# One decode step of an adaLN attention block: keys and values as one stream of 53 transfers, sums by transposes, the last wo row like the others

## The chip, the core and the metric

The kernel runs on one core of a Trainium2 chip. A core has a matrix engine (TensorE, "PE", with weight loads shown as "PEld"), a vector engine (VectorE, "DVE"), a scalar engine (ScalarE, "ACT"), a general engine (GpSimd, "POOL"), and a queue engine (SyncE, "SP") that here issues all transfers; 16 DMA engines move the data. The on-chip memory (SBUF) has 128 partitions; matmul results go to PSUM. The metric is the device time of one execution in microseconds, as the median of several. The profile shows one execution, from its first to its last instruction (its span).

## What is computed

One token (D = 640) goes through an adaptive-layernorm block: attention over a cache of 8192 positions with 32 heads of 192, then a squared-ReLU MLP with 1536 hidden units. All is fp32.

```python
mod = (silu(c) @ w_mod).reshape(6, 640)
sa, ca, ga, sb, cb, gb = mod
h = layernorm(x) * (1 + ca) + sa
q = (h @ wq).reshape(32, 192)
scores = einsum("hd,hkd->hk", q, k_cache) * 192 ** -0.5
o = einsum("hk,hkd->hd", softmax(scores), v_cache)
x = x + ga * (o.reshape(32 * 192) @ wo)
h = layernorm(x) * (1 + cb) + sb
x = x + gb * (relu(h @ w1 + b1) ** 2 @ w2 + b2)
```

The two caches are 201 MB each and every byte is read once; all weights together are some 49 MB.

## The kernel before

**Streaming.** Everything comes through three SBUF slots (`slot`, L54) of 14,208 words per partition, used in turn. A transfer into a slot waits until what was in it is used up. The order on SP is: the first weights `wm0`, then for each head its keys (`load_k`) and its values (`load_v`), then the remaining weights `wm1`, `w1`, `gb`, `w2` (L312 to L319). The keys of a head are 64 positions per partition, each of 192 words. Behind the keys of most heads lies a piece of weights in the same transfer: `wq` for the next pair of heads behind the even ones, `wo` of the pair before behind the odd ones. The last two heads' keys come in two and in four pieces (`CUTS`), the values of head 31 are behind the `wo` of the last pair.

**Keys** (`keys`, L192). For one half of a head's positions at a time, DVE multiplies the keys by the query that every partition holds (L201, in place); POOL folds the last 7/16 of the positions, adding the upper 96 words of each to the lower 96 (L203); DVE meanwhile sums the other 9/16 (L204), then the folded ones (L205). That gives one score per position.

**Softmax** (`softmax`, L216). DVE takes the maximum in each partition (L218), PE spreads it over all partitions by a matmul with the identity (L220), DVE takes the maximum of that (L222), and ACT computes the exponentials with their sum in each partition (L228). After an odd head PE adds the two heads' sums over the partitions with a matmul with ones (`total`, L97).

**Values** (`values`, L233). The positions go 8 at a time: 8 steps, each 3 matmuls of a 32-column group with 512 columns of values (L240). An fp32 matmul shows as two instructions in the profile, so a head is 48. The useful eighth of the result is picked by a mask in `project` (L254, L256), which one pair later also divides by the sum, and turns the row into columns by a matmul with `quad` (L258). `attend` (L260) multiplies it with the pair's piece of `wo`: 6 matmuls of 320 columns in two column groups, accumulated in `att_a` over the pairs; for the last pair 12 of 160 columns in four column groups, on top of `att_a` that `gather` (L275) had already brought into place while the keys of head 31 were still being worked on.

**The end.** The modulation rows 3 and 4 are computed by `mod` in steps, placed between the parts of the second layernorm (the `between` of `layernorm`, L107; `mod_b`, L326). Row 2 is done before the values of head 31 (L308). Then follow the first MLP matrix (L343), bias, ReLU and square (L346 to L348), the row 5 (`mod`, L351) and two rounds of matmuls whose result nobody reads (`WARM`, L353 to L355), the second MLP matrix (L363), and the result (L366 to L368).

All engines run their instructions in the order in which the program writes them.

Of the kernel before, what the change touches and what calls it, by code (L numbers as in the profile page):

```python
# [8 lines left out]
F32 = mybir.dt.float32  # L9
# [22 lines left out]
CUTS = {("k", H - 2): 2, ("k", H - 1): 4}  # L32
WO = 3 * D
WQ = KB * PW
HD = NPOS * DH
SLOT = HD + WO
WITHOUT_W = (1, H - 2)
WITH_W = tuple(h for h in range(H) if h not in WITHOUT_W)
W1_CUT = ((0, 3), (3, 2))
W2_CUT = ((0, 6), (6, 3), (9, 1), (10, 1), (11, 1))  # L40
WARM = 2
EPS = 1e-5


@with_exitstack
def block_kernel(ctx: ExitStack, tc: tile.TileContext, kw, ky, vc, wm0, wm1, w1, gb, w2, out):
# [18 lines left out]
    quad = const.tile([P, 32 * NV], F32, name="quad")  # L65
    nc.vector.memset(quad, 0.0)
    for g in range(NV):
        nc.vector.memset(quad[32 * g:32 * (g + 1), 32 * g:32 * (g + 1)], 1.0)
# [31 lines left out]
    def layernorm(x, copies, scale1, shift, name, between=lambda: None):  # L100
# [6 lines left out]
        between()  # L107
# [24 lines left out]
    def mod(first, n, w, steps=(KB,)):  # L132

        ps = psum.tile([P, 512], F32, tag="q", name=f"ps_mod{first}", bufs=2)
        b = 0
        for k in steps:
            for b in range(b, b + k):
                wb = w[:, b].rearrange("p (m n) -> p m n", m=n)
                for g in range(G):
                    nc.tensor.matmul(ps[32 * g:32 * (g + 1), :n * DG], e[:, b:b + 1].to_broadcast([P, 32]),  # L140
                                     wb[:, :, DG * g:DG * (g + 1)], start=(b == 0), stop=(b == KB - 1))
            b += 1
            if b < KB:
                yield
        nc.vector.tensor_copy(mods[:, first:first + n], ps[:, :n * DG].rearrange("p (m n) -> p m n", m=n))  # L145
        yield

    qb_t, k_t, v_t = {}, {}, {}

    def load(src, to, h, what):  # L150
        to[h] = slot(f"{what}{h}")
        n, w = CUTS.get((what, h), 1), src.shape[1]
        for c in range(n):
            a, b = c * HD // n, (c + 1) * HD // n if c + 1 < n else w
            nc.sync.dma_start(to[h][:, a:b], src[:, a:b])

    def load_k(h):

        load(kw[WITH_W.index(h)] if h in WITH_W else ky[WITHOUT_W.index(h)], k_t, h, "k")

    def load_v(h):
        load(vc[h], v_t, h, "v")

    load_k(0)
    next(mod(0, 2, wm0_t[:, :KB * 2 * D].rearrange("p (b n) -> p b n", b=KB)))
# [8 lines left out]
    hR = const.tile([P, KB, P], F32, name="hR")  # L174
    nc.vector.tensor_copy(hR, h1[:, :, None].to_broadcast([P, KB, P]))

    def query(i, w):
        w = w.rearrange("p (b n) -> p b n", b=KB)
        ps = psum.tile([P, 512], F32, tag="q", name=f"ps_q{i}", bufs=2)
        for b in range(KB):  # L180
            nc.tensor.matmul(ps[:, :PW], hR[:, b], w[:, b], start=(b == 0), stop=(b == KB - 1))  # L181
        qb_t[i] = work.tile([P, PW], F32, name=f"qb{i}", tag="qb")
        nc.scalar.activation(qb_t[i], ps[:, :PW], AF.Copy, scale=DH ** -0.5)  # L183
# [3 lines left out]
    att_s = const.tile([P, 2 * DG], F32, name="att_s")  # L187
    nc.vector.memset(att_s, 0.0)
    att_t = []
    query(0, wm0_t[:, KB * 2 * D:KB * 2 * D + WQ])  # L190

    def keys(h, between):  # L192

        q = qb_t[h // 2][:, DH * (h % 2):DH * (h % 2 + 1)]
        sc = work.tile([P, NPOS], F32, tag="sc", name=f"sc{h}")
        t = k_t[h][:, :HD].rearrange("p (i d) -> p i d", d=DH)
        n = NPOS // max(2, CUTS.get(("k", h), 1))
        m = n - POOL * n // 16
        for c in range(NPOS // n):
            pr, s = t[:, c * n:(c + 1) * n], sc[:, c * n:(c + 1) * n]  # L200
            nc.vector.tensor_mul(pr, pr, q[:, None, :].to_broadcast([P, n, DH]))  # L201
            half = pr[:, m:, :DH // 2]
            nc.gpsimd.tensor_add(half, half, pr[:, m:, DH // 2:])  # L203
            nc.vector.tensor_reduce(s[:, :m], pr[:, :m], axis=AX.X, op=ALU.add)  # L204
            nc.vector.tensor_reduce(s[:, m:], half, axis=AX.X, op=ALU.add)  # L205
            between(c)
        return sc
# [3 lines left out]
    def inverse(i):  # L211
        r = work.tile([P, 2], F32, tag="r", name=f"r{i}")
        nc.vector.reciprocal(r, sum_t.pop(i))
        ri_t[i] = r

    def softmax(h, sc):  # L216
        mp = work.tile([P, 1], F32, tag="mp", name=f"mp{h}")
        nc.vector.tensor_reduce(mp, sc, axis=AX.X, op=ALU.max)  # L218
        ps = psum.tile([P, 512], F32, tag="sm", name=f"ps_mx{h}", bufs=2)
        nc.tensor.matmul(ps[:, :P], mp.to_broadcast([P, P]), ident, start=True, stop=True)  # L220
# [3 lines left out]
        p = work.tile([P, NPOS, 32 // E], F32, tag="p", name=f"p{h}", bufs=1)  # L224
# [3 lines left out]
        nc.scalar.activation(p, sc[:, :, None].to_broadcast([P, NPOS, 32 // E]), AF.Exp, bias=nm, accum_out=sp[:, h % 2:h % 2 + 1])  # L228
        if h % 2:
            sum_t[h // 2] = total(sp, f"sum{h // 2}")  # L230
        return p

    def values(h, p):  # L233

        t = v_t.pop(h)[:, :HD].rearrange("p (j g n) -> p j g n", g=NV, n=E * ED)
        ps_t[h] = psum.tile([P, 512], F32, tag="o", name=f"ps_o{h}", bufs=3)
        n = NPOS // E
        for j in range(n):
            for g in range(NV):
                nc.tensor.matmul(ps_t[h][32 * g:32 * (g + 1)], p[:, E * j:E * (j + 1)].rearrange("p e r -> p (e r)"),  # L240
                                 t[:, j, g], start=(j == 0), stop=(j == n - 1))
# [3 lines left out]
    def project(i):  # L245
# [3 lines left out]
        inverse(i)  # L249
        r2 = ri_t.pop(i)  # L250
        for a in range(2):
            h = 2 * i + a
            om = work.tile([P, ED, E], F32, tag="om", name=f"om{h}", bufs=1)
            nc.vector.scalar_tensor_tensor(om[:n], ps_t.pop(h)[:n].rearrange("p (d e) -> p d e", e=E), r2[:n, a:a + 1],  # L254
                                           mask[:n, None, :].to_broadcast([n, ED, E]), op0=ALU.mult, op1=ALU.mult)
            nc.vector.tensor_reduce(os_[:n, a], om[:n], axis=AX.X, op=ALU.add)  # L256
        os_t[i] = psum.tile([P, 512], F32, tag="sm", name=f"ps_oT{i}", bufs=2)
        nc.tensor.matmul(os_t[i][:, :n], os_[:n].rearrange("p a d -> p (a d)"), quad[:n], start=True, stop=True)  # L258

    def attend(i, w):  # L260
        oT = work.tile([P, 96], F32, tag="oT", name=f"oT{i}")
        nc.vector.tensor_copy(oT, os_t.pop(i)[:, :96])  # L262
        w = w.rearrange("p (j n) -> p j n", j=3)
        if i + 1 < NPAIR:
            for j in range(3):
                for g in range(2):
                    nc.tensor.matmul(att_a[32 * g:32 * (g + 1), :2 * DG], oT[:, 32 * j:32 * (j + 1)],  # L267
                                     w[:, j, 2 * DG * g:2 * DG * (g + 1)], start=(i == 0 and j == 0), stop=(i == NPAIR - 2 and j == 2))
            return
# [141 lines left out]
```

## Time and profile before

| | |
|---|---|
| device time, median of 3 runs | 1057.9 us (1057.46 to 1057.91) |
| span of the profiled execution (its device time is not shown by itself) | 1055.5 us |
| DVE busy | 831.4 us (79%) |
| PE busy | 463.7 us (44%) |
| POOL busy | 194.8 us (18%) |
| bytes read from HBM | 451.82 MB |
| mean granted TensorE clock | 0.694 of full speed |

In the profile, a group of instructions is named by its line, its engine and what it writes and reads, with its count, busy time and the mean of one in ns. In the view of the stretches, the columns after the stretch are its length, the busy time (and number of instructions) of PE, PEld, DVE, ACT and POOL, the granted TensorE clock, the busy share of the DMA engines and the GB/s that they moved. In the timeline, a row is a start, the time until the last of its instructions ended, engine, line and operation, and in brackets the idle time before it and what ended that.

### The profile page before, as it was taken

The numbers are of one execution on the slowest core, as the hardware profiler recorded it, in microseconds if no ns is written. First come the engines' busy times: TensorE is split into PE (matmuls) and PEld (weight loads), VectorE is DVE, ScalarE is ACT, GpSimd is POOL, SyncE is SP. The second block draws the span as 40 slices with busy tenths as digits, with TensorE's granted clock in tenths as the row PEclk, the third lists the DMA queues.
The fourth block names the chain that finished last, engine by engine and source line by source line (L and its number), as shares of the span: only waits on it lengthen the run. The fifth ranks groups of instructions, "written<-read, shape, count | busy, mean of one in ns | idle before, by whom it ended". The sixth has DMA issues, their size and how long they took to land.

```text
span 1055.5 us, 5687 instructions
## 1 busy us (share of the span) xinstructions
PE 463.7 (44%) x2356; PEld 155.0 (15%) x2356; DVE 831.4 (79%) x409; ACT 33.4 (3%) x88; POOL 194.8 (18%) x72
## 2 busy tenths in 40 slices
PE   3234443355543345463334534335453335535446
PEld 1101111111111111120111111101111111111113
DVE  2886878978787987878888687997878798789963
ACT  1000000000000000000000000000000000000000
POOL 0211112211212221212221212221221221122110
PEclk9667666766666766666676666666666666767769
DMA  9999999999999999999999999999999999999997
GB/s 403 435 434 428 432 440 427 441 424 437 433 433 428 440 424 441 424 439 427 431 437 437 422 442 430 428 439 426 439 429 433 428 438 433 434 427 432 424 426 310
DMA packets 11410, 452.18 MB, mean 428 GB/s; under 512 B 1269, under 2 KB 1273, under 8 KB 1785
## 3 DMA queue, kind: packets, MB, share of 16 engines
q1 hardware_dynamic: 11384, 451.83, 99.3%
q8 instruction: 18, 0.29, 0.1%
q14 instruction: 8, 0.06, 0.0%
HBM read 451.82 MB, written 0.00 MB: 428 GB/s over the span
## 4 chain that ended last, share of the span: by engine, by line
DMA 42%; DVE 39%; PE 17%; ACT 1%; issue 1%; SPq 0%; DVEq 0%; ACTq 0%
DMA k<-in_kw 36%; DVE k L201 21%; PE ps_o L240 14%; DVE sc L204 12%; DVE sc L205 5%; DMA k<-in_ky 3%; DMA w_t<-in_w 2%; PE ps_mx L220 1%; DMA wm_t<-in_wm 1%; ACT p L228 1%; PE ps_sum L97 1%; PE ps_mod L140 1%; PE ps_q L181 1%; DVE nm L222 0%; DVE mp L218 0%
## 5 line engine op out<-in xcount | busy, mean ns | idle before, releaser
L201 DVE TENSOR_TENSOR k<-k,qb 128x6144 f32<-128x6144 f32 (+1 forms) x66 | 419.7, 6359 | 141.6 <-DMA k<-in_kw 134.4
L203 POOL TENSOR_TENSOR k<-k 128x1344 f32<-128x1344 f32 (+1 forms) x66 | 194.1, 2941 | 820.9 <-DVE k L201 476.1
L240 PE MATMUL ps_o<-v,p 128*32 128x512 f32 x1536 | 290.4, 731 | 17.2 <-ACT p L228 17.2
L204 DVE TENSOR_REDUCE sc<-k 128x18 f32<-128x3456 f32 (+1 forms) x66 | 240.5, 3644 | 4.3
L220 PE MATMUL ps_mx<-ident,mp 128*128 128x128 f32 x64 | 25.5, 501 | 416.2 <-DVE mp L218 416.2
L240 PEld LDWEIGHTS ps_o<-v,p 128*32 128x32 f32 x1536 | 68.4, 131 | 215.4 <-issue 193.1
L267 PE MATMUL att_a<-k,oT 128*32 128x320 f32 x180 | 49.6, 720 | 114.2 <-DVE oT L262 113.1
L205 DVE TENSOR_REDUCE sc<-k 128x14 f32<-128x1344 f32 (+1 forms) x66 | 99.0, 1500 | 0.0
L220 PEld LDWEIGHTS ps_mx<-ident,mp 128*128 128x128 f32 x64 | 16.1, 312 | 442.8 <-DVE mp L218 421.0
L181 PE MATMUL ps_q<-k,hR 128*128 128x384 f32 x150 | 52.3, 496 | 0.0
L228 ACT ACTIVATE p<-sc,nm 128x256 f32<-128x256 f32 x32 | 16.2, 508 | 760.6 <-DVE nm L222 496.9
L267 PEld LDWEIGHTS att_a<-k,oT 128*32 128x32 f32 x180 | 13.7, 161 | 136.7 <-DVE oT L262 116.7
L222 DVE TENSOR_REDUCE nm<-ps_mx 128x1 f32<-128x128 f32 x32 | 9.3, 291 | 28.5 <-PE ps_mx L220 28.5
L181 PEld LDWEIGHTS ps_q<-k,hR 128*128 128x128 f32 x150 | 27.3, 190 | 27.9 <-issue 11.7
L254 DVE SCALAR_TENSOR_TENSOR om<-ps_o,r,mask 96x512 f32<-96x512 f32 x32 | 23.9, 747 | 6.5 <-PE ps_o L240 5.4
L256 DVE TENSOR_REDUCE os<-om 96x64 f32<-96x512 f32 x32 | 21.8, 682 | 1.1
L140 PE MATMUL ps_mod<-wm_t,silu 128*32 128x320 f32 (+1 forms) x120 | 11.7, 550 | 14.6 <-DVE silu L128 14.6
L97 PE MATMUL ps_sum<-sp,ones 128*128 128x2 f32 x32 | 9.4, 364 | 17.2 <-ACT p L228 17.2
L183 ACT ACTIVATE qb<-ps_q 128x384 f32<-128x384 f32 x16 | 7.9, 491 | 195.2 <-PE ps_q L181 195.2
L97 PEld LDWEIGHTS ps_sum<-sp,ones 128*128 128x128 f32 x32 | 8.0, 312 | 21.9 <-ACT p L228 21.9
L145 DVE COPY mods<-ps_mod 128x320 f32<-128x320 f32 (+1 forms) x4 | 1.6, 398 | 10.2 <-PE ps_mod L140 10.2
L76 DVE COPY small<-wm_t 128x27 f32<-128x27 f32 x1 | 0.2, 179 | 11.2 <-DMA wm_t<-in_wm 11.2
(77 smaller groups left out, 90.9 us busy)
## 6 DMA issues: line engine op xcount, KB each, us to landing
k<-in_kw SPq DMA_DIRECT2D x29, 7104.0 KB, 27.4
v<-in_vc SPq DMA_DIRECT2D x32, 6144.0 KB, 22.1
k<-in_ky SPq DMA_DIRECT2D x1, 6144.0 KB, 28.3
k<-in_ky SPq DMA_DIRECT2D x2, 3072.0 KB, 21.5
k<-in_kw SPq DMA_DIRECT2D x3, 1536.0 KB, 15.5
wm_t<-in_wm SPq DMA_DIRECT2D x1, 4173.5 KB, 12.7
wm_t<-in_wm SPq DMA_DIRECT2D x1, 3200.0 KB, 29.3
wm_t<-in_wm SPq DMA_DIRECT2D x1, 2560.0 KB, 18.2
```

What stands on the lines that cost most here:

```text
L97: nc.tensor.matmul(ps[:, :n], ones, src, start=True, stop=True)
L140: nc.tensor.matmul(ps[32 * g:32 * (g + 1), :n * DG], e[:, b:b + 1].to_broadcast([P, 32]), wb[:, :, DG * g:DG * (g + 1)], start=(b == 0), s ...
L181: nc.tensor.matmul(ps[:, :PW], hR[:, b], w[:, b], start=(b == 0), stop=(b == KB - 1))
L201: nc.vector.tensor_mul(pr, pr, q[:, None, :].to_broadcast([P, n, DH]))
L203: nc.gpsimd.tensor_add(half, half, pr[:, m:, DH // 2:])
L204: nc.vector.tensor_reduce(s[:, :m], pr[:, :m], axis=AX.X, op=ALU.add)
L205: nc.vector.tensor_reduce(s[:, m:], half, axis=AX.X, op=ALU.add)
L220: nc.tensor.matmul(ps[:, :P], mp.to_broadcast([P, P]), ident, start=True, stop=True)
L228: nc.scalar.activation(p, sc[:, :, None].to_broadcast([P, NPOS, 32 // E]), AF.Exp, bias=nm, accum_out=sp[:, h % 2:h % 2 + 1])
L240: nc.tensor.matmul(ps_t[h][32 * g:32 * (g + 1)], p[:, E * j:E * (j + 1)].rearrange("p e r -> p (e r)"), t[:, j, g], start=(j == 0), stop=( ...
L254: nc.vector.scalar_tensor_tensor(om[:n], ps_t.pop(h)[:n].rearrange("p (d e) -> p d e", e=E), r2[:n, a:a + 1], mask[:n, None, :].to_broadca ...
L267: nc.tensor.matmul(att_a[32 * g:32 * (g + 1), :2 * DG], oT[:, 32 * j:32 * (j + 1)], w[:, j, 2 * DG * g:2 * DG * (g + 1)], start=(i == 0 an ...
```

## The change

The caches and the `wq` and `wo` pieces lie in one array in the order in which they are used. A planner (`plan`) cuts it into 53 transfers for the same three slots, which grow to 16,128 words per partition. Each transfer holds some keys (mostly 44 positions), mostly 5 steps of values (a head has 8), and at times a piece of `wq` (now 512 columns, 12 pieces in all) or of `wo`. Transfer 51 holds the last 30 positions of keys, 5 steps of values and the `wo` of pair 14; transfer 52 holds only the last 7 steps of values. The loop goes over transfers: values whose exponentials are there come first on PE, then the keys of the transfer as a whole, and values whose head was only finished in this transfer (`late`) at its end. The transfer three places ahead is asked for at the end of each step.

What follows the caches is `wm1` in two transfers, `w1` with `gb` in two and `w2` in three. With `wm0` and the output that is 62 transfers; before there were 80.

The maximum and the sum of a head go over the partitions by PE transposes in place of matmuls; the sum is finished by a DVE reduce. The division moves from the masking to the column form, in the new function `turn`. `attend` treats all pairs alike: three matmuls of 512 columns into the column group 96 to 127, and one matmul of 384 columns that covers the other 128 columns of all three parts in 96 output rows. `gather` comes at the end, after the last `attend` and after `mod(2, 3)`, which computes the rows 2 to 4 in one go. Row 5 is computed by `gate`, and one unread matmul remains of the eight.

```diff
-CUTS = {("k", H - 2): 2, ("k", H - 1): 4}
+QC = 512
+SLOT = 84 * DH
+VPC = 5
+W1_CUT = (3 * FF, KB * FF + KB * D)
+W2_CUT = (8 * D, 11 * D, 12 * D)
+WM_CUT = (WO + 9 * D, WO + 15 * D)
+WARM = 1
...
+def plan():
+    chunks, kp, vp, q, o = [], 0, 0, 1, 0
+    while kp < H * NPOS or vp < H * NPOS // E:
+        room, w = SLOT, []
...
+            nk = min(H * NPOS - kp, (room - VPC * UNIT) // DH)
+            nv = min(H * NPOS // E - vp, (room - nk * DH) // UNIT)
+            while nv and ((vp + nv - 1) // (NPOS // E) + 1) * NPOS > kp + nk:
+                nv -= 1
+            nk = min(H * NPOS - kp, (room - nv * UNIT) // DH)
+        chunks.append((kp, nk, vp, nv, w))
...
+def gate(m, w):
...
+        for k in range(2):
+            nc.tensor.matmul(ps[64 * k:64 * (k + 1), :2 * DG], e[:, b:b + 1].to_broadcast([P, 64]),
+                             w[:, b, 2 * DG * k:2 * DG * (k + 1)], start=(b == 0), stop=(b == KB - 1))
+    for g in range(G):
+        r = slice(32 * g, 32 * (g + 1))
+        nc.scalar.activation(mods[r, m], ps[r, DG * (g % 2):DG * (g % 2 + 1)], AF.Copy)
...
-        nc.tensor.matmul(ps[:, :P], mp.to_broadcast([P, P]), ident, start=True, stop=True)
+        nc.tensor.transpose(ps[:, :P], mp.to_broadcast([P, P]), ident)
...
-            sum_t[h // 2] = total(sp, f"sum{h // 2}")
+            nc.scalar.activation(wide, sp[:, :, None].to_broadcast([P, 2, ED]), AF.Copy)
+            nc.tensor.transpose(ps[:, :P], wide.rearrange("p a d -> p (a d)"), ident)
...
-        nc.tensor.matmul(os_t[i][:, :n], os_[:n].rearrange("p a d -> p (a d)"), quad[:n], start=True, stop=True)
+        nc.tensor.transpose(os_t[i][:, :n], os_[:n].rearrange("p a d -> p (a d)"), ident[:n, :n])
+
+    def turn(i):
+        nc.vector.tensor_reduce(oT, os_t[i][:, :96].rearrange("p (j r) -> p j r", j=NV), axis=AX.X, op=ALU.add)
+        nc.vector.tensor_scalar(oT, oT, ri_t.pop(i), None, op0=ALU.mult)
...
     def attend(i, w):
+        nc.scalar.activation(oW, oT[:, :, None].to_broadcast([P, NV, 32]), AF.Copy)
+        for j in range(NV):
+            nc.tensor.matmul(att_a[96:, :512], oT[:, j:j + 1].to_broadcast([P, 32]), w[:, j, :512],
+                             start=(first and j == 0), stop=(last and j == NV - 1))
+        nc.tensor.matmul(att_a[:96, :NV * (D - 512)], oW.rearrange("p j r -> p (j r)"), w[:, :, 512:],
+                         start=first, stop=last)
...
     def gather():
+        nc.vector.tensor_copy(att_s[96:, :512], att_a[96:, :512])
+        for j in range(NV):
+            r = slice(32 * j, 32 * (j + 1))
+            nc.scalar.activation(att_s[r, 512:], att_a[r, (D - 512) * j:(D - 512) * (j + 1)], AF.Copy)
...
+    for n, (kp, nk, vp, nv, extra) in enumerate(PLAN):
...
+        for v in range(vp, vp + nv):
+            if v not in late:
+                values(vt[:, v - vp], v)
+        if nk:
+            multiply(kt, kp, nk)
+            m = nk - POOL * nk // 16
+            half = kt[:, m:, :DH // 2]
+            nc.gpsimd.tensor_add(half, half, kt[:, m:, DH // 2:])
...
+            project(project_now)
+        if nk:
+            scores(kt[:, :m], kp)
+        if project_now is not None:
+            turn(project_now)
+        if wo_t is not None:
+            attend(*wo_t)
+        if nk:
+            scores(half, kp + m)
+        if done is not None:
+            softmax(done)
...
+        for v in late:
+            values(vt[:, v - vp], v)
...
+        load(n + 3)
...
     project(NPAIR - 1)
+    turn(NPAIR - 1)
     attend(NPAIR - 1, wm1_t[:, :WO])
-    mod_b = mod(3, 2, wm1_t[:, WO + KB * D:WO + KB * 3 * D].rearrange("p (b n) -> p b n", b=KB), (2, 2, 1))
-    next(mod_b)
+    mod(2, 3, wm1_t[:, WO:WO + KB * 3 * D].rearrange("p (b n) -> p b n", b=KB))
...
-    nc.vector.tensor_mul(x1, att_t[0][:, :DG], mods[:, 2])
+    nc.vector.tensor_mul(x1, gather()[:, :DG], mods[:, 2])
...
-    next(mod(5, 1, gb_t))
+    gate(5, gb_t)
...
-        for g in range(G):
-            nc.tensor.matmul(idle[32 * g:32 * (g + 1)], ones[:, :32], w1_t[:, k, :512], start=True, stop=True)
+        nc.tensor.matmul(idle, ones, w1_t[:, k, :512], start=True, stop=True)
```

289 lines of the change are left out of this document (146 added, 143 removed).

## The prediction

> **What bounds the kernel now.** I read the page first, then the stretches, then the timeline of the end.
>
> ```profile
> span 1055.5 us, 5687 instructions
> DMA  9999999999999999999999999999999999999997
> GB/s 403 435 434 428 432 440 427 441 424 437 433 433 428 440 424 441 424 439 427 431 437 437 422 442 430 428 439 426 439 429 433 428 438 433 434 427 432 424 426 310
> q1 hardware_dynamic: 11384, 451.83, 99.3%
> ```
>
> The DMA engines are busy in every slice but the last, 99.3% of the span, so up to the end the kernel is one uninterrupted stream. DVE, at 79%, keeps up with it. The change reads the same bytes (caches, and weights of the same size cut otherwise). It can win only by a higher rate or a shorter end, and lose by holes in the stream or a longer end.
>
> ```profile
> 437.00:499.00 62.00, 27.48 (x129) 8.76 (x126) 50.71 (x22) 1.69 (x5) 12.10 (x4) 0.67 1.01 436
> 626.00:688.00 62.00, 26.21 (x129) 8.64 (x126) 50.79 (x22) 1.69 (x5) 12.10 (x4) 0.72 0.99 428
> 1030.00:1040.00 10.00, 5.89 (x81) 3.00 (x82) 5.40 (x16) 0.26 (x1) 0.00 (x0) 1.00 1.00 422
> ```
>
> Two heads' worth of time moves 428 to 436 GB/s (the last column), with the DMA share at 0.99 and 1.01: the rate is that of busy engines, not of waiting ones. Near the end it is 422. I use 432 in what follows. The end in the timeline:
>
> ```profile
> 1017.38 0.22 DVE L218 TENSOR_REDUCE mp<-sc 128x1 f32<-128x64 f32 x1
> 1018.87 0.51 ACT L228 ACTIVATE p<-sc,nm 128x256 f32<-128x256 f32 x1 [16.44 <-DVE nm L222]
> 1019.53 0.59 PE L97 MATMUL ps_sum<-sp,ones 128*128 128x2 f32 x2 [1.07 <-ACT p L228]
> 1022.71 7.50 PE L240 MATMUL ps_o<-v,p 128*32 128x512 f32 x48
> 1031.06 0.68 DVE L256 TENSOR_REDUCE os<-om 96x64 f32<-96x512 f32 x1
> 1031.79 0.46 PE L258 MATMUL ps_oT<-quad,os 96*128 96x96 f32 x2 [1.58 <-DVE os L256]
> 1032.60 1.02 PE L272 MATMUL att<-wm_t,oT 128*32 128x160 f32 x24 [0.35 <-DVE oT L262]
> 1033.44 1.26 PE L140 MATMUL ps_mod<-wm_t,silu 128*32 128x320 f32 x16
> 1034.05 0.33 DVE L330 TENSOR_TENSOR x<-x,x_t 128x160 f32<-128x160 f32 x1
> 1037.03 0.16 DVE L117 RECIPROCAL ln_rs<-ln_sd 128x1 f32<-128x1 f32 x1 [0.95 <-ACT ln_sd L115]
> 1037.96 0.24 DVE L335 TENSOR_SCALAR cb<-mods 128x160 f32<-128x160 f32 x1
> 1039.02 0.34 DVE L82 STREAM_TRANSPOSE hT<-ln_h 128x160 f32<-128x160 f32 x1
> 1039.47 5.13 PE L343 MATMUL ps_f<-w_t,hT 128*32 128x384 f32 x40 [2.10 <-issue]
> 1044.38 1.57 PE L140 MATMUL ps_mod<-w_t,silu 128*32 128x160 f32 x40
> 1045.74 1.93 PE L355 MATMUL ps_warm<-w_t,ones 128*32 128x512 f32 x16
> 1047.46 3.16 PE L363 MATMUL ps_y<-w_t,fT 128*32 128x160 f32 x80
> 1051.71 0.48 PE L363 MATMUL ps_y<-w_t,fT 128*32 128x160 f32 x8 [0.31 <-DMA w_t<-in_w]
> 1052.97 0.65 SPq L368 DMA_DIRECT2D out_y<-y  x1
> ```
>
> The values of head 31 end at 1030.2 (1022.71 + 7.50), the first MLP matrix starts at 1039.5, and the last block of the second starts when its weights land, at 1051.7. Before that PE waited hardly at all: the work after the last head takes about as long as the weights that still stream in. So the end is balanced: there is almost no slack on either side, and whatever lengthens the work after the last values lengthens the whole.
>
> **The change part by part.**
>
> *Stream.* Behind transfer 51, the last with keys, come 7 steps of values (5.51 MB), `wm1` (5.90), `w1` with `gb` (5.57) and `w2` (3.93): 20.9 MB, at 432 GB/s 48.4 us. If the last weights land at 1051.7 as before, transfer 51 lands at 1003.3; by 422 GB/s it is 1002.2. I take 1003. That there are 62 transfers and not 80 I cost at nothing, since the share of busy engines shows no hole between them now; this is the subject of the second rival.
>
> *The middle.* Keys of a transfer of 44 positions, from these rows:
>
> ```profile
> L201 DVE TENSOR_TENSOR k<-k,qb 128x6144 f32<-128x6144 f32 x62 | 406.3, 6553 | 141.6 <-DMA k<-in_kw 134.4 <-ACT qb L183 4.4 <-DMA k<-in_ky 2.8
> L204 DVE TENSOR_REDUCE sc<-k 128x18 f32<-128x3456 f32 x62 | 232.7, 3753 | 4.1
> L203 POOL TENSOR_TENSOR k<-k 128x1344 f32<-128x1344 f32 x62 | 187.7, 3027 | 797.0 <-DVE k L201 452.1 <-issue 344.8
> L205 DVE TENSOR_REDUCE sc<-k 128x14 f32<-128x1344 f32 x62 | 95.7, 1543 | 0.0
> L254 DVE SCALAR_TENSOR_TENSOR om<-ps_o,r,mask 96x512 f32<-96x512 f32 x32 | 23.9, 747 | 6.5 <-PE ps_o L240 5.4
> L256 DVE TENSOR_REDUCE os<-om 96x64 f32<-96x512 f32 x32 | 21.8, 682 | 1.1
> ```
>
> Multiply 44/32 x 6.55 = 9.0, sum of the first 25 positions 25/18 x 3.75 = 5.2, of the 19 folded ones 19/14 x 1.54 = 2.1: 16.3 us, and 17.7 with a softmax (from mp at 1017.38 to the second maximum, 1.4). A transfer of 8.26 MB takes 19.1. POOL's fold, 19/14 x 3.03 = 4.1, lies under the 5.2. Transfers with a `project` have fewer keys or borrow a little: two times 0.75 + 0.68, 2.9 us, on top of 34 positions' 12.6 and the softmax. So DVE follows the stream, and a slot is free some 20 us after it landed, where the stream needs it only after two more transfers, 38 us. Holes in the middle: none, cost 0. This cover is gone if DVE falls behind by over 15 us; at worst, waiting 5 us for PE in every pair, it has 2 x (23.7 + 1.4) + 2.9 + 5 = 58 us of work for two heads against 62.8.
>
> *The last head.* Transfer 51 (30 keys, `wo` of pair 14, the `project` of pair 14), from its landing: multiply 30/32 x 6.55 = 6.1; project 2.9; sum of 17 positions 3.5; `turn`, two small DVE operations, at most the 0.25 of the row below each, 0.5. Then `attend` on PE, ahead of the softmax's transpose in PE's order. This is a new form: three 512-column matmuls that all use one column group, so none can run beside another, and one of 384. The nearest rows are the query's matmuls, which also run alone, once at a low clock and once at a higher one:
>
> ```profile
> 24.75 6.25 PE L181 MATMUL ps_q<-wm_t,hR 128*128 128x384 f32 x10 [1.93 <-DVE hR L175]
> 30.84 3.39 PE L181 MATMUL ps_q<-k,hR 128*128 128x384 f32 x10
> L262 DVE COPY oT<-ps_oT 128x96 f32<-128x96 f32 x16 | 4.0, 248 | 0.9 <-PE ps_oT L258 0.9
> L145 DVE COPY mods<-ps_mod 128x320 f32<-128x320 f32 x2 | 1.0, 492 | 5.9 <-PE ps_mod L140 5.9
> L145 DVE COPY mods<-ps_mod 128x160 f32<-128x160 f32 x2 | 0.6, 306 | 4.2 <-PE ps_mod L140 4.2
> L280 PE MATMUL att<-att_s,ident 128*32 128x160 f32 x8 | 0.5, 311 | 0.5 <-ACT att_s L277 0.5
> ```
>
> A 384-column instruction is 0.34 (fast) or 0.63 us (slow), a 512-column one by proportion 0.45 or 0.83; `attend`, with its 6 + 2, is 3.4 or 6.3. In mid-stream the clock is between (0.67 and 0.72 in the stretches above), so 4.8, under which the 1.4 of folded sums disappear. Then the softmax: end of mp to the end of exp, 1.8 (1017.60 to 1019.38); the sum's transpose and the copy before it, 1.1; and all 8 steps of values, 7.5 as measured, since 7 of them have landed by then (transfer 52 lands 12.7 us after 51). Sum 6.1 + 2.9 + 3.5 + 0.5 + 4.8 + 1.8 + 1.1 + 7.5 = 28.2. The values end at 1003 + 28.2 = 1031.2, a microsecond later than now. The transposes are priced as the matmuls that they replace; their bounds are nothing and that. The Trainium skill ("TensorE: Matmul & The Clock Gate", Terms) calls the transpose mode four times faster for fp32; the three on this path would then give back about 1.3 us, an estimate, and no row of before shows one.
>
> *From the values to the first MLP matrix.* Now 9.3 us (1030.2 to 1039.5). After: mask and sum of head 31, 1.5 (until 1031.74), and transpose 0.5, as now; `turn` 0.5; `attend` 3.4 where 1.02 stood (PE's clock here is 1.00 in the stretch 1030 to 1040, so the fast value). Then `mod(2, 3)`, now in front of everything else and no longer between the layernorm's steps: 40 instructions of 480 columns; 16 of 320 took 1.26, so 1.5 x 40/16 x 1.26 = 4.7, less the end latency, 4.4; its copy to SBUF, by the two rows 0.68. DVE only then copies `att_a`'s 512 columns, 0.7; `gather`'s 8 small matmuls 0.5; product and sum 0.7. The layernorm, from 1034.38 to 1037.19 and from 1037.96 to 1039.36, is 4.2 without the wait for the rows. With eight handovers of 0.1 that is 17.4. The added 8.1 are the whole loss: what ran under the stream (the gathering, row 2) or under the layernorm (rows 3 and 4) now stands in the chain.
>
> *From there to the end.* First MLP matrix to the start of the second now 8.0 (1039.47 to 1047.46). `gate` has half as many column groups at work, 10 rounds of 320 columns at 0.27 = 2.7 in place of 1.6; one unread matmul alone, 0.9 in place of 1.9: 8.1 after. The second matrix, with all its weights there, 96 instructions at 3.16/80 = 3.8. From its end (1052.19) to the span's end 3.3. Together 15.2. ACT's four copies of the gate lie under the second matrix.
>
> Sum: 1003 + 28.2 + 17.4 + 15.2 = 1063.8 of span. The span shown is 2.4 below the median of the runs, 1057.9; so **1066 us**, 0.8% slower. The weights have then long landed; a late `w1` (its slot is freed by the step of values of transfer 51 that waits for head 31, about 22 us after landing, with 23.5 needed to leave no hole) costs nothing until it is 6 us late.
>
> **The rivals.**
>
> *PE at half clock.* The same chain, but with PE's idle times longer than now, `attend` 6.3 both times, the values at 16 rounds of 0.83 = 13.3, `mod` 8.3 by the first `mod`'s pace (doubling 4.4 less what overlaps, 8). That is +1.5 +5.8 +2.9 +3.6, of which a half is likelier than all: 1066 + 9 = **1075**. For it: 0.67 in mid-stream. Against: 1.00 at the same place now.
>
> *The stream becomes faster.* With 18 transfers fewer and longer rows the engines might lose less at the boundaries. Its place is everything before transfer 51, 430.9 MB. At 438 GB/s this takes 983.8 in place of 997.5 us: **1052**. Below 437 it isn't enough to be faster. For it: single slices at 440. Against: these stand next to slices of 424, and no stretch of 62 us is above 436, with the engines busy throughout. The Trainium skill ("DMA: Bandwidth & Descriptors", Where 436 GB/s comes from) puts the ceiling of the 16 ports at 435.2 GB/s; by it this rival ends at about 1059, no change. The stretch of 436 agrees with it within what its edges cut.
>
> *Between these* lies a rate of 434 to 436, or a shorter chain by 6 us: no change.
>
> **How the numbers follow.** The forecast 0.62, half clock 0.17, the faster stream (or a chain as short) 0.15, between 0.06. No change means within 0.2%, 1055.8 to 1060.0, about what a measurement of this kernel can tell. Slower is 0.62 + 0.17 = 0.79. The forecast's own range: low, `attend` fast in transfer 51 (-1.4), transposes at nothing (-1.8), the first MLP matrix at full clock, 3.2 (-1.9), 1002.2 for the landing: 1060; high, half of the first rival: 1071. The range for 8 in 10 reaches further to both sides, 1057 to 1074, leaving about 0.13 below and 0.07 above.
>
> **What would show it.** In the changed profile: a DMA share of 9 in all slices but the last two, and the last slices much emptier than now; the last keys' multiply starting within 2 us of 1003; exponentials of head 31 near 1023 and values to 1031; `attend` of 3 to 6 us with rounds that don't overlap; `mod` of 4 to 5 us between it and the gathering; the first MLP matrix at 1048 to 1049, and the second running without a wait for DMA. It is wrong if the second matrix still waits for its last weights, if the stream shows holes or another rate, or if the last keys start late because DVE has fallen behind.

## The result, and the profile after

The changed kernel takes 1063.78 us (median of four runs, 1063.51 to 1064.96) against 1057.82 before (1057.46 to 1057.91): a ratio of 1.0059, 95% interval 1.0045 to 1.0074. It is slower by 6 us. 1066 was forecast, in a range of 1057 to 1074. The profiled run took 1063.51, with a span of 1061.7.

The page of the changed kernel, in its first lines, the line of DMA slices and the costliest group of DVE:

```profile
span 1061.7 us, 5129 instructions
...
PE 489.0 (46%) x2102; PEld 131.6 (12%) x2102; DVE 831.9 (78%) x431; ACT 43.7 (4%) x122; POOL 188.4 (18%) x58
...
DMA  9999999999999999999999999999999999999994
GB/s 407 429 433 452 426 433 428 431 435 442 428 433 426 433 435 441 430 431 425 439 432 440 430 431 430 436 430 438 433 435 430 433 426 436 436 437 428 427 418 190
...
q1 hardware_dynamic: 8792, 451.83, 98.5%
...
L240 DVE TENSOR_TENSOR chunk<-chunk,qb 128x6528 f32<-128x6528 f32 (+15 forms) x82 | 419.8, 5150 | 133.9 <-DMA chunk<-in_kv 133.9
```

The stream has no hole in the middle: 9 in every slice but the last. DVE waits for landings for 133.9 us, as long as it did for keys before (134.4), so it has not fallen behind. The last slice is emptier than before (4 at 190 GB/s, where it was 7 at 310): the weights are all there, and work goes on without them.

The same stretch of 880 us, first after, then before (columns as in the prediction's stretches):

```profile
60.00:940.00 880.00, 404.53 (x1597) 104.08 (x1591) 718.31 (x341) 30.17 (x91) 166.40 (x47) 0.70 1.00 433
```

```profile
60.00:940.00 880.00, 386.98 (x1774) 123.28 (x1771) 714.02 (x308) 23.70 (x70) 169.47 (x56) 0.68 1.00 433
```

The same 433 GB/s at a DMA share of 1.00. TensorE has 177 instructions less in it and is busy 18 us longer, which costs nothing here, since DMA is the limit. Now the end, in the timeline of the changed kernel:

```profile
1001.04 6.16 DVE L240 TENSOR_TENSOR chunk<-chunk,qb 128x5760 f32<-128x5760 f32 x1 [0.92 <-DMA chunk<-in_kv]
...
1013.90 4.17 PE L320 MATMUL att_a<-chunk,oT 128*32 128x512 f32 x6 [3.59 <-DVE oT L310]
...
1018.00 1.12 PE L322 MATMUL att_a<-chunk,oW 128*96 128x384 f32 x2
...
1018.96 0.27 PE L264 MATMUL ps_mx<-ident,mp 128*128 128x128 f32 x1
1019.35 0.29 DVE L266 TENSOR_REDUCE nm<-ps_mx 128x1 f32<-128x128 f32 x1 [3.89 <-PE ps_mx L264]
...
1020.66 0.33 PE L277 MATMUL ps_sum<-ident,wide 128*128 128x128 f32 x1 [1.43 <-ACT wide L275]
...
1020.92 7.07 PE L289 MATMUL ps_o<-chunk,p 128*32 128x512 f32 x48
...
1029.51 0.30 PE L305 MATMUL ps_oT<-ident,os 96*128 96x96 f32 x1 [1.52 <-DVE os L303]
...
1030.42 2.76 PE L320 MATMUL att_a<-wm_t,oT 128*32 128x512 f32 x6 [0.61 <-DVE oT L310]
...
1033.11 0.89 PE L322 MATMUL att_a<-wm_t,oW 128*96 128x384 f32 x2
...
1033.93 4.23 PE L171 MATMUL ps_mod<-wm_t,silu 128*32 128x480 f32 x40
...
1038.23 0.66 DVE L173 COPY mods<-ps_mod 128x480 f32<-128x480 f32 x1 [7.86 <-PE ps_mod L171]
1038.92 0.70 DVE L327 COPY att_s<-att_a 32x512 f32<-32x512 f32 x1
...
1039.71 0.83 ACT L330 ACTIVATE att_s<-att_a 32x128 f32<-32x128 f32 x3 [9.03 <-DVE att_s L327]
...
1040.59 0.46 PE L333 MATMUL att<-att_s,sel 128*32 128x160 f32 x2 [0.45 <-ACT att_s L330]
...
1046.03 4.99 PE L413 MATMUL ps_f<-w_t,hT 128*32 128x384 f32 x40 [1.85 <-DVE hT L116]
1050.96 2.91 PE L180 MATMUL ps_mod<-w_t,silu 128*64 128x320 f32 x20
...
1053.80 1.12 PE L424 MATMUL ps_warm<-w_t,ones 128*128 128x512 f32 x2
...
1054.86 3.47 PE L432 MATMUL ps_y<-w_t,fT 128*32 128x160 f32 x96
```

Head 31's values end at 1027.99 (1020.92 + 7.07), 2.2 us before they did in the old kernel (1030.2). But the first MLP matrix starts at 1046.03 in place of 1039.47: from values to matrix it takes 18.0 us and not 9.3. In those 18 us stand the longer `attend`, `mod`, its copy and the gathering, one after the other. The second matrix runs all 96 instructions without a wait for weights. Their issues and the longest landing in the changed kernel (the first row: time in ns, first and last start; the second: KB and us from issue to landing):

```profile
L201 SPq DMA_DIRECT2D w_t<-in_w x5: 328/424/425, 1022.0 to 1028.9; - x5
```

```profile
w_t<-in_w SPq DMA_DIRECT2D x1, 320.0 KB, 20.7
```

The last weights land at 1028.9 + 20.7 = 1049.6, 5.3 us before the second matrix starts. Before, that matrix waited for them until 1051.7. The kernel has changed its bound at the end: from the stream to the chain of work behind the last head. The 6.2 us of span add up along that chain: 2.2 less until the values end, 8.8 more from there to the first MLP matrix, 0.8 more to the second matrix, 1.3 less in it, since it no longer waits, and 0.1 more behind it.

### The profile page after: what moved, and what is told of

The parts are those of the page before. It is cut to its first block, busy times and chain, and to the rows that moved or that the text cites. A ratio compares the mean times of both kernels' runs of the same rounds, so it can differ in the third digit from the quotient of the medians.

```text
span 1061.7 us, 5129 instructions
## 1 busy us (share of the span) xinstructions
PE 489.0 (46%) x2102; PEld 131.6 (12%) x2102; DVE 831.9 (78%) x431; ACT 43.7 (4%) x122; POOL 188.4 (18%) x58
## 3 DMA queue, kind: packets, MB, share of 16 engines
q1 hardware_dynamic: 8792, 451.83, 98.5%
## 4 chain that ended last, share of the span: by engine, by line
DMA 57%; DVE 32%; PE 10%; ACT 1%; issue 0%; SPq 0%; DVEq 0%; ACTq 0%
DMA chunk<-in_kv 57%; DVE chunk L240 17%; DVE sc L248 13%; PE ps_o L289 5%; PE att_a L320 2%; DVE os L303 1%; ACT p L272 1%; DVE om L301 1%; PE ps_mx L264 0%; PE ps_f L413 0%; PE att_a L322 0%; PE ps_mod L171 0%; PE ps_sum L277 0%; DVE nm L266 0%; PE ps_y L432 0%
## 5 line engine op out<-in xcount | busy, mean ns | idle before, releaser
L240 DVE TENSOR_TENSOR chunk<-chunk,qb 128x6528 f32<-128x6528 f32 (+15 forms) x82 | 419.8, 5150 | 133.9 <-DMA chunk<-in_kv 133.9
L248 DVE TENSOR_REDUCE sc<-chunk 128x19 f32<-128x1824 f32 (+16 forms) x111 | 334.0, 3042 | 0.4
L364 POOL TENSOR_TENSOR chunk<-chunk 128x1824 f32<-128x1824 f32 (+7 forms) x52 | 187.7, 3610 | 821.3 <-DVE chunk L240 567.7
L289 PE MATMUL ps_o<-chunk,p 128*32 128x512 f32 x1536 | 292.5, 727 | 59.5 <-DMA chunk<-in_kv 44.6
L264 PE MATMUL ps_mx<-ident,mp 128*128 128x128 f32 x32 | 14.1, 439 | 316.9 <-DVE mp L262 316.9
L289 PEld LDWEIGHTS ps_o<-chunk,p 128*32 128x32 f32 x1536 | 66.0, 129 | 258.7 <-issue 179.7
L320 PE MATMUL att_a<-chunk,oT 128*32 128x512 f32 x90 | 65.0, 882 | 48.4 <-DVE oT L310 48.4
L221 PE MATMUL ps_q<-chunk,ln_h 128*128 128x512 f32 x110 | 63.4, 734 | 42.1 <-DMA chunk<-in_kv 42.1
L221 PEld LDWEIGHTS ps_q<-chunk,ln_h 128*128 128x128 f32 x110 | 25.5, 240 | 79.4 <-DMA chunk<-in_kv 46.0
L301 DVE TENSOR_TENSOR om<-ps_o,mask 96x512 f32<-96x512 f32 x32 | 21.9, 683 | 6.0 <-PE ps_o L289 5.2
L322 PE MATMUL att_a<-chunk,oW 128*96 128x384 f32 x30 | 14.4, 562 | 0.0
## 6 DMA issues: line engine op xcount, KB each, us to landing
wm_t<-in_wm SPq DMA_DIRECT2D x1, 4493.5 KB, 13.7
```

Of the source, the lines that this page charges most:

```text
L221: nc.tensor.matmul(ps, h1[:, b:b + 1].to_broadcast([P, P]), w[:, b], start=(b == 0), stop=(b == KB - 1))
L248: nc.vector.tensor_reduce(sc[:, a % SRING:a % SRING + b - a], src[:, a - first:b - first], axis=AX.X, op=ALU.add)
L264: nc.tensor.transpose(ps[:, :P], mp.to_broadcast([P, P]), ident)
L301: nc.vector.tensor_mul(om[:n], ps_t.pop(h)[:n].rearrange("p (d e) -> p d e", e=E), mask[:n, None, :].to_broadcast([n, ED, E]))
L320: nc.tensor.matmul(att_a[96:, :512], oT[:, j:j + 1].to_broadcast([P, 32]), w[:, j, :512], start=(first and j == 0), stop=(last and j == NV ...
L322: nc.tensor.matmul(att_a[:96, :NV * (D - 512)], oW.rearrange("p j r -> p (j r)"), w[:, :, 512:], start=first, stop=last)
```

## The experiments

All are edits of the changed kernel; ratios are to the kernel before, whose median beside them lay between 1057.69 and 1057.82.

**1. Rows 2 to 4 back into the gaps.** My theory puts 4 to 5 us of the loss on `mod(2, 3)` standing whole in the chain; the rival is that moved rows save nothing because something else is late in their place. The edit puts row 2 under the mask and sum of the last head, and rows 3 and 4 between the steps of the layernorm (`mod` becomes a generator, which the diff leaves out: each `next` issues all five blocks of its weights, or as many as the numbers at its end say, and the last one also the copy).

```diff
...
+    mod_a = mod(2, 1, wm_t[:, :, :D])
+    next(mod_a)
     project(NPAIR - 1)
+    next(mod_a)
     turn(NPAIR - 1)
     attend(NPAIR - 1, wm1_t[:, :WO])
-    mod(2, 3, wm1_t[:, WO:WO + KB * 3 * D].rearrange("p (b n) -> p b n", b=KB))
+    mod_b = mod(3, 2, wm_t[:, :, D:], (2, 2, 1))
...
+    att = gather()
+    next(mod_b)
...
     def scale_b():
+        next(mod_b)
+        next(mod_b)
...
-    hT2 = columns(layernorm(x1, 32, scale_b, lambda: mods[:, 3], "ln2"), DG, "hT2")
+    hT2 = columns(layernorm(x1, 32, scale_b, lambda: mods[:, 3], "ln2", lambda: next(mod_b)), DG, "hT2")
```

> Kernel after, but the modulation rows are computed as in the kernel before: row 2 while DVE masks the last values, rows 3 and 4 in steps between the parts of the layernorm. Theory (the chain behind the last values sets the end): the 4.2 us of matmuls and the 0.7 us copy leave the chain, at most 0.8 comes back as waits in the layernorm; the span goes from 1061.7 to about 1057.5 and the ratio to before from 1.006 to about 1.002. Rival (the stream or DVE set the end, and the chain only follows): within 1 us of 1061.7.

Measured: 1059.69 (ten runs, 1056.68 to 1060.84), ratio 1.0014 [1.0004, 1.0023], span 1057.5. The rows in its timeline that show the move:

```profile
1027.65 1.53 PE L174 MATMUL ps_mod<-wm_t,silu 128*32 128x160 f32 x38
...
1041.71 5.12 PE L427 MATMUL ps_f<-w_t,hT 128*32 128x384 f32 x40 [2.05 <-DVE hT L116]
```

Row 2 runs at 1027.65, while DVE masks and sums, and the first MLP matrix starts 4.3 us earlier than in the changed kernel (1041.71 against 1046.03). The span is shorter by 4.2. So the place of the rows is worth what the theory said, and nothing else was late in their stead. It is two thirds of the 6 us (4.1 us by the medians, with intervals apart).

**2. The gathering early, the last `attend` short.** The sums of fifteen pairs are copied out while the last head's values run, and put in place by PE right behind them; the last pair is added directly to the result by 24 instructions of 160 columns in four column groups.

```diff
+        if i == NPAIR - 1:
+            for j in range(NV):
+                for g in range(G):
+                    nc.tensor.matmul(att[32 * g:32 * (g + 1), :DG], oT[:, j:j + 1].to_broadcast([P, 32]),
+                                     w[:, j, DG * g:DG * (g + 1)], start=False, stop=(j == NV - 1))
+            return
...
+    att = gather()
     project(NPAIR - 1)
...
-    nc.vector.tensor_mul(x1, gather()[:, :DG], mods[:, 2])
+    nc.vector.tensor_mul(x1, att[:, :DG], mods[:, 2])
```

> Kernel after, but the sums of the pairs 0 to 14 are brought into place before the last project, and the last attend is 12 matmuls of 160 columns in four column groups. Theory: 2.2 us of gathering (from the copy of the rows to the product) and 2.5 of attend's 3.5 us leave the chain; the span goes to about 1057, ratio about 1.0015. Rival (PE's time is hidden there): within 1 us of 1061.7.

Measured: 1061.21 (seven runs, 1060.21 to 1061.95), ratio 1.0031 [1.0020, 1.0042], span 1059.6: faster than the changed kernel, but 2.6 us of what was expected is missing. The timeline of this kernel, then two of its stretches:

```profile
1030.63 1.46 PE L319 MATMUL att<-wm_t,oT 128*32 128x160 f32 x24 [0.61 <-DVE oT L310]
...
1031.84 5.52 PE L171 MATMUL ps_mod<-wm_t,silu 128*32 128x480 f32 x40
...
1042.85 6.02 PE L420 MATMUL ps_f<-w_t,hT 128*32 128x384 f32 x40 [1.85 <-DVE hT L116]
```

```profile
1032.00:1034.00 2.00, 2.00 (x16) 0.50 (x12) 0.00 (x0) 0.00 (x0) 0.00 (x0) 0.50 1.04 448
...
1044.00:1046.00 2.00, 2.00 (x16) 0.59 (x12) 0.00 (x0) 0.00 (x0) 0.00 (x0) 0.50 0.93 388
```

`attend` is short, but takes 1.46 where the same 24 instructions took 1.02 before; the same `mod` takes 5.52 where it took 4.23, and the first MLP matrix 6.02 for 4.99. The granted clock (the third number from the end) is 0.50 where the changed kernel shows, at the same time:

```profile
1032.00:1034.00 2.00, 2.00 (x9) 0.43 (x11) 0.00 (x0) 0.00 (x0) 0.00 (x0) 1.00 0.99 426
```

So a new theory: the shorter chain works, and a lower clock behind its gaps takes 2.8 us of it back (0.44 + 1.29 + 1.03). The rival: the instructions are slower for another reason (their data, their place), and the clock only goes with it. The gap ahead of `attend` is not new: it is 2.4 us in the changed kernel and 2.2 here, so why the clock falls only here is a question of its own, taken up in the last section.

**3. The same with the gaps filled.** Unread matmuls of 512 columns go where PE waits: one after the gathering, two after `mod`, three in the layernorm.

```diff
+    def fill(n):
+        for _ in range(n):
+            fills.append(psum.tile([P, 512], F32, tag="sm", name=f"ps_fill{len(fills)}", bufs=2))
+            nc.tensor.matmul(fills[-1], ones, att_s[:, :512], start=True, stop=True)
...
     att = gather()
+    fill(1)
...
     mod(2, 3, wm1_t[:, WO:WO + KB * 3 * D].rearrange("p (b n) -> p b n", b=KB))
+    fill(2)
```

> The kernel with the early gathering and the short last attend (span 1059.6), and six matmuls of ones with 512 columns whose result nobody reads, in the gaps of PE behind the last values and in the layernorm. That kernel lost 1.3 us in the rows' matmuls (5.5 instead of 4.2) and 1.0 in the first MLP matrix (6.0 instead of 5.0). Theory (PE's clock falls in the gaps that the shorter attend leaves): the rows take 4.2 again, the first MLP matrix 3.2 to 3.6, span about 1055.5. Rival (the longer times have another source, such as data that land late, or the added matmuls only stand in the way): 1059 or more.

Measured: 1057.36 (ten runs, 1055.62 to 1058.42), ratio 0.9998 [0.9988, 1.0007], span 1056.3. Timeline and stretches:

```profile
1032.20 4.21 PE L182 MATMUL ps_mod<-wm_t,silu 128*32 128x480 f32 x40
...
1042.13 3.43 PE L433 MATMUL ps_f<-w_t,hT 128*32 128x384 f32 x40
```

```profile
1032.00:1034.00 2.00, 2.00 (x32) 0.84 (x28) 0.00 (x0) 0.00 (x0) 0.00 (x0) 1.00 1.08 464
...
1044.00:1046.00 2.00, 2.00 (x24) 0.73 (x18) 0.37 (x1) 0.00 (x0) 0.00 (x0) 1.00 0.98 408
```

The clock is 1.00 in both stretches, `mod` is back at 4.21, and the first MLP matrix takes 3.43. Work that nobody reads makes this kernel 3.85 us faster (1061.21 to 1057.36, intervals apart). The clock theory holds; the rival, in which the data or the place slows the instructions, falls, since these are the same. The MLP matrix gains more than was lost to experiment 2 (3.43, where the changed kernel took 4.99), because the changed kernel itself runs most of it at a clock of 0.50.

**4. `attend` ahead of the sums of scores.** In transfer 51 the softmax's transpose stands behind `attend` on PE (DVE has the maximum at 1015.45, the transpose starts at 1018.96). If that wait costs what it shows, starting `attend` earlier, under DVE's sums, gives it back.

```diff
-        if nk:
-            scores(kt[:, :m], kp)
         if project_now is not None:
             turn(project_now)
         if wo_t is not None:
             attend(*wo_t)
+        if nk:
+            scores(kt[:, :m], kp)
```

> Kernel after, but turn and attend of a pair come before the sums of the keys of their transfer, for all pairs. Theory: attend then runs under the sums, the second maximum of head 31 no longer waits 3.9 us for PE, and 0.6 us are paid for DVE's wait for the transpose; the span goes to about 1058.5, ratio about 1.003. Rival (the last values wait for their transfer or the stream sets the end): within 1 us of 1061.7.

Measured: 1062.08 (four runs, 1060.36 to 1063.06), ratio 1.0039 [1.0024, 1.0054], span 1061.3.

```profile
1016.74 0.29 DVE L266 TENSOR_REDUCE nm<-ps_mx 128x1 f32<-128x128 f32 x1 [0.49 <-PE ps_mx L264]
...
1018.32 8.76 PE L289 MATMUL ps_o<-chunk,p 128*32 128x512 f32 x48
```

```profile
1018.00:1022.00 4.00, 3.94 (x16) 1.10 (x19) 1.72 (x4) 0.01 (x1) 0.00 (x0) 0.57 0.96 411
```

The maximum is there 2.6 us earlier (1016.74 against 1019.35), as expected. The values start 2.6 earlier but take 8.76 in place of 7.07: the clock in their first stretch is 0.57, where it is 1.00 in the first 4 us of the changed kernel's values (1021 to 1025). Of the 2.6 us 0.9 is left (they end at 1027.08, not 1027.99), and of that 0.4 in the span: the first MLP matrix starts 0.9 earlier, but the clock comes back to 1.00 only at 1049.28 (1049.23 in the changed kernel), so it takes 5.47 and not 4.99. The 3.2 us that were expected did not come. By its number the rival's mark is met (within 1 us of 1061.7), though not for its reason, and the interval of the ratio overlaps that of the changed kernel.

**5. The same with two unread matmuls,** behind `attend` and behind the maximum's transpose.

```diff
             attend(*wo_t)
+        if n == len(PLAN) - 2:
+            fill(1)
...
+        if h == H - 1:
+            fill(1)
```

> The kernel with turn and attend before the sums (span 1061.3), and in transfer 51 two matmuls of ones with 512 columns whose result nobody reads, one behind attend and one behind the transpose of the maximum. In that kernel the exponentials of head 31 came 2.6 us sooner, but its 8 steps of values took 8.8 us and not 7.1. Theory (PE's clock fell in the 3.5 us between attend and the values): the values take 6.7 to 7.1 again, and end at about 1025.3; the span is about 1059 if the clock in the end stays as it was, ratio about 1.002. Rival (the values are slower for another reason): they take 8.5 or more, span 1061 or more.

Measured: 1061.05 (six runs, 1060.19 to 1062.52), ratio 1.0035 [1.0022, 1.0047], span 1059.5.

```profile
1018.52 7.07 PE L297 MATMUL ps_o<-chunk,p 128*32 128x512 f32 x48
```

```profile
1018.00:1022.00 4.00, 3.73 (x28) 1.17 (x31) 1.72 (x4) 0.21 (x1) 0.00 (x0) 1.00 0.93 396
```

The values take 7.07 again, at a clock of 1.00, and end at 1025.59. In the trace the 2.4 us are there; the two medians (1062.08 and 1061.05) have intervals that overlap, so the time itself doesn't prove it.

**6. All three edits (1, 2 and 4) together,** without unread matmuls: rows 2 to 4 then fill the gaps themselves. The gathering goes ahead of row 2.

```diff
+    att = gather()
     wm_t = wm1_t[:, WO:WO + KB * 3 * D].rearrange("p (b n) -> p b n", b=KB)
     mod_a = mod(2, 1, wm_t[:, :, :D])
     next(mod_a)
     project(NPAIR - 1)
```

> The three edits together. Theory: 4.2 + 4.7 + 3.3 = 12 us leave the chain, more than it is longer than the stream; then the last weights set the end again, which land at about 1048.5, and the span is about 1052.5, under the kernel before: ratio about 0.997. If only the chain counted, 1049.5. Rival (stream or DVE): within 1 us of 1061.7.

Measured: 1055.95 (ten runs, 1055.28 to 1056.46), ratio 0.9982 [0.9972, 0.9991], span 1054.3. It beats both kernels, by 7.8 us and by 1.8 us. The span is still 1.8 us longer than expected. A wait that the expectation did not have stands in the second of these rows:

```profile
1035.95 2.14 PE L433 MATMUL ps_f<-w_t,hT 128*32 128x384 f32 x24 [2.05 <-DVE hT L116]
...
1040.46 2.52 PE L433 MATMUL ps_f<-w_t,hT 128*32 128x384 f32 x16 [2.37 <-DMA w_t<-in_w]
```

The first MLP matrix now starts at 1035.95, 10 us earlier than in the changed kernel, and waits 2.37 us for the second transfer of `w1`: the chain has become as short as the stream. Behind that wait the clock is lower (0.63 from 1040 to 1043), and `gate` takes 3.53 for 2.91. The last weights, which were expected at 1048.5, land at 1049.7 (issued at 1026.7, 23.0 to the landing).

**7. `w1` in three transfers,** so that its last blocks don't wait for `gb`.

```diff
-W1_CUT = (3 * FF, KB * FF + KB * D)
+W1_CUT = (3 * FF, KB * FF, KB * FF + KB * D)
```

> The three edits together (span 1054.3) and w1 without gb in its second transfer, gb in a third. In the three edits together the first MLP matrix waits 2.4 us for that transfer, until 1040.5. Theory: it now lands 3.8 us sooner, at about 1036.7, before it is needed; the first MLP matrix ends at about 1039, the second matrix's last block waits for its weights at about 1048.5, and the span is about 1052.3, ratio about 0.9965. Rival (the chain has no slack left anywhere, or the wait moves to gb): 1054 or more.

Measured: 1055.53 (ten runs, 1055.28 to 1057.28), ratio 0.9984 [0.9974, 0.9993], span 1053.8: no difference from the last one that can be told.

```profile
1046.88 3.53 PE L452 MATMUL ps_y<-w_t,fT 128*32 128x160 f32 x96 [2.13 <-DMA w_t<-in_w]
```

The first matrix no longer waits; the second does, 2.13 us, for the first piece of `w2`. The wait has only moved, as the rival said, though to `w2` and not to `gb`; the span lies between the two expectations, next to the rival's 1054. With the last weights at 1049.9 (issued at 1027.2, 22.7 to the landing) the stream sets the end again, as it did before the change.

**8. Each transfer of the caches as two.** The forecast put transfer 51 at 1003, and it landed at 1001. This tests whether fewer transfers speed up the stream, as my second rival said, by making their number twice as large.

```diff
-            pieces = [(kv[start[n]:start[n] + P * m].rearrange("(p n) -> p n", p=P), (m,))]
+            pieces = [(kv[start[n]:start[n] + P * m].rearrange("(p n) -> p n", p=P), (m // 2, m))]
```

> Kernel after, but each of the 53 transfers is issued as two of half the width, one behind the other. Transfer 51 landed at 1001.0 where I had worked out 1003.0. Theory that each transfer costs the stream something: 2 us for some 11 transfers fewer ahead of it are 0.18 us each, so 53 more make the last keys' multiply start at about 1010 and the span about 1070. Rival (the number of transfers is free and the two microseconds have another source): the multiply starts within 0.6 us of 1001.0, and the time is that of the kernel after within 1.5 us.

Measured: 1065.04 (four runs, 1062.60 to 1066.39), ratio 1.0067 [1.0052, 1.0082], span 1064.6. The multiply that waits for the whole of transfer 50, first in the changed kernel (where one row holds two instructions), then in this one:

```profile
982.90 9.03 DVE L240 TENSOR_TENSOR chunk<-chunk,qb 128x1920 f32<-128x1920 f32 x2 [2.69 <-DMA chunk<-in_kv]
```

```profile
986.67 6.96 DVE L240 TENSOR_TENSOR chunk<-chunk,qb 128x6528 f32<-128x6528 f32 x1 [0.62 <-DMA chunk<-in_kv]
```

```profile
w_t<-in_w SPq DMA_DIRECT2D x1, 320.0 KB, 23.9
```

Transfer 50 is there 3.8 us later, with 51 boundaries more; the last weights land at 1029.6 + 23.9 = 1053.5, 3.9 later. In the other seven edits transfer 50 is there within 0.5 us of the changed kernel, and so are the last weights, so this is no scatter. It is 0.075 us a transfer, between the two expectations. By it the 18 transfers that the change saves give 1.35 us. A transfer comes with its packets (11,384 before, 8,792 after, 16,424 here, some 144 more for each), and whether the transfer or its packets cost the time the runs do not separate.

The time shows none of this: the intervals of this kernel and the changed one overlap, and 1065.04 is within the rival's 1.5 us. The last keys lie in the first half of their transfer, and their multiply (at 1001.75, 0.7 later, just outside the rival's 0.6) no longer waits for a landing but stands behind the softmax of head 30 on DVE. The span grew by 2.9 mostly through another thing: the last `attend` ran at a lower clock, 4.46 for 2.76.

## Why the prediction was right

The span is forecast as 1063.8 and was 1061.7. By the terms of the sum:

| term | forecast | measured |
|---|---|---|
| transfer 51 lands | 1003 | 1001.04 |
| last head, to the end of its values | 28.2 | 26.95 |
| values to first MLP matrix | 17.4 | 18.04 |
| first matrix to second | 8.1 | 8.83 |
| second matrix | 3.8 | 3.47 |
| to the end of the span | 3.3 | 3.37 |

The landing accounts for 2.0 of the 2.1 us by which the span was forecast too long. The other rows agree in the sum only by luck: they miss by -1.25, +0.64, +0.73, -0.33 and +0.07, which cancel. The signs named beforehand came in the order forecast, 2 to 3 us early: exponentials at 1020.2, values to 1028.0, the first MLP matrix at 1046.0.

**The mechanism was right.** The forecast called the 8.1 us added between values and first matrix the whole loss; they came as 8.8. Experiment 1 moves only the rows and gets 4.2 us of span back; experiments 1, 2 and 4 together get 7.4, more than the 6.2 that were lost. That the weights would have landed long before, and that the second matrix would run without a wait, both came out.

**The middle was right.** DVE's work per pair did not make holes, and the same stretch moves the same 433 GB/s.

**The stream was sized 2 us too late.** The forecast set the cost of 18 transfers at nothing, because the share of busy engines showed no holes. Experiment 8 shows that a boundary of this stream costs 0.075 us, too little to show in shares given to a hundredth: 1.35 of the 2 us, if the smaller transfers of before cost the same. The rest stays open; 1 GB/s in 433 over the whole stream is 2.3 us, below what the stretches resolve. The second rival was thus right in kind, and too large by a factor of over six: it had 13.7 us.

**The transposes were priced too high.** I took the matmuls that they replace. The groups of both kernels, before and then after:

```profile
L220 PE MATMUL ps_mx<-ident,mp 128*128 128x128 f32 x64 | 25.5, 501 | 416.2 <-DVE mp L218 416.2
```

```profile
L264 PE MATMUL ps_mx<-ident,mp 128*128 128x128 f32 x32 | 14.1, 439 | 316.9 <-DVE mp L262 316.9
```

Before, 64 instructions for 32 heads, two each; now 32, one each and no longer. In busy time that is 14.1 against 25.5, a bit more than half. On the last head and behind it, the step from the end of `attend` to the start of the values, forecast at 1.8 + 1.1, took 1.8 (1019.12 to 1020.92); a part of that is that the first transpose starts 0.16 before the end of `attend` that the profile gives. The values took 7.07 for 7.5: before the change the clock was 0.50 in their first 0.9 us (until 1023.6), and here it is 1.00 throughout. The Trainium skill's fourfold gain ("TensorE: Matmul & The Clock Gate", Terms) does not show in these rows, which give 1.8 times in busy time.

**Three sizes were too low, and one sum.** The parts of the 17.4 add up to 17.9 with their eight handovers, so against its own parts this term missed by 0.1: what the gathering took more came back in the transpose (0.30 for 0.5), in `mod` (4.23 for 4.4) and in shorter handovers. The handover in the gathering was missed: the three copies of ACT wait for DVE's copy of another part of the same tile (the row at 1039.71, idle 9.03 until L327), and the last two of the gathering's matmuls wait for them, so that the gathering takes 1.38 and not 0.5. The first stretch of the MLP is 0.7 longer (`gate` 2.91 for 2.7, the unread matmul 1.12 for 0.9, the handovers the rest). `attend` in transfer 51 took 5.2 for 4.8.

**Half clock, the first rival,** did not come where it was priced highest: the clock is 1.00 during the last values and from 1032 to 1036, as the forecast argued from the same place in the old kernel. In other places it was there: 0.50 from 1016 to 1018, in `attend` of transfer 51, and from 1043 to 1049, in the first MLP matrix, where it had been in part before the change too. Experiments 2, 4 and 8 met it in further places, and each lost 1.7 to 2.8 us to it. The price of this rival does not follow from its parts: they add up to 13.8, of which a half is 6.9, and the 9 that was added is two thirds.

## What to carry to other kernels

Where the last transfers and the work behind them end together, price every instruction by what hides it in its place: TensorE's fewer instructions were worth nothing here under a stream that sets the pace, and the 40 of `mod` that came to stand in the chain cost 4 us. After a repair, read the end again for its bound: when the chain had become 7 us shorter, the next wait was the weights', and finer cuts only moved it. When work on PE is shortened or moved forward, compare the granted clock of what follows before trusting the difference of the instructions.

## What the runs showed of the hardware

**The clock can fall after a short gap.** In experiment 2 PE ran only a transpose of 0.30 between the end of its gathering (1028.47) and `attend` (1030.63), and the clock was 0.50 from 1031.1 on. The Trainium skill ("TensorE: Matmul & The Clock Gate", Part 1: The HAM clock gate) has the gate close after an idle window of about 3.4 us; here 2.2 us with a transpose inside were enough.

**The same gap does not always cost, and the traces show why.** From the end of the values to the last `attend` it is 2.4 us both in the changed kernel and in experiment 8, with the same instructions in it; one then shows 2.76 for `attend`'s six, the other 4.46. In all ten traces the clock changes only at points that lie a whole number of steps of 3.41 us apart: cut at these points from 200 to 1050 us, none of some 250 steps in each trace mixes two clocks. What counts is how long PE was busy within a step. The step ahead of a fall in experiment 2 and the step behind it, the step ahead of a fall in experiment 8, and the step with the same gap in the changed kernel (PE's busy time is the second number behind the stretch):

```profile
1027.66:1031.07 3.41, 1.55 (x27) 0.74 (x25) 1.85 (x4) 0.00 (x0) 0.00 (x0) 1.00 1.00 421
1031.07:1034.48 3.41, 3.41 (x36) 1.50 (x28) 0.00 (x0) 0.00 (x0) 0.00 (x0) 0.50 1.05 450
```

```profile
1028.30:1031.71 3.41, 1.28 (x7) 0.37 (x4) 1.85 (x4) 0.28 (x1) 0.00 (x0) 1.00 1.02 433
```

```profile
1028.75:1032.16 3.41, 2.04 (x5) 0.60 (x6) 1.17 (x3) 0.28 (x1) 0.00 (x0) 1.00 1.04 447
```

In the changed kernel a boundary between two steps falls into the gap and splits it, so that neither step is idle enough. Over the ten traces a step at full clock with less than 1.39 us of PE work was always followed by one at 0.50, and one with more than 1.65 never; between them it went either way. A step at 0.50 was followed by a faster one only with 2.65 or more.

Kernels whose end is set by PE's chain also spread more from run to run (experiment 1: 4.2 us over ten runs; the kernel before beside it: 0.9 over 22). That this comes from where the steps fall in each run is likely by the above and not shown: each kernel has one trace.

**A transfer in a full stream costs 0.075 us,** its packets included, where transfers of some 8 MB are cut in two (experiment 8).
